# Queries of a pooled-attention and expert-attention kernel loaded as two head halves, with the whole order written anew

## The chip, the cores and the metric

One core of a Trainium2 chip. The metric is the device time of one execution in microseconds, lower is better; the kernel before has a median of 171.48 us over 4 runs (171.14 to 173.48).

## What is computed

Two stages on 8 batches of 576 tokens. Stage one is attention of 8 heads of width 64 in which keys and values are first averaged over 8 neighbours, so that 72 pooled keys remain. Its output, the 8 heads side by side, is the 512-wide input x of stage two: four causal attention "experts" with one head each of width 64, of which a gate picks two for each token.

```
k_p = k.reshape(B, H, Sp, pool, D).mean(axis=3)          # pool = 8, Sp = 72
v_p = v.reshape(B, H, Sp, pool, D).mean(axis=3)
attn = softmax(scale * q @ k_p^T);  x = attn @ v_p       # heads side by side: B x 576 x 512
...
logits = x @ w_gate                                      # 4 experts, the best 2 kept, softmax over them
for e in range(E):
    q, k, v = x @ wq[e], x @ wk[e], x @ wv[e]
    a = softmax(causal(scale * q @ k^T))
    out += (w of e, or 0) * (a @ v @ wo[e])
```

## The kernel before

**An order written out.** The program is a list of some 1,040 tokens, the string SEQ (from L550). A loop at the end of the kernel reads one token after the other and records its instructions; each engine then runs its own instructions in just that order, and semaphores carry what depends on other engines. A token is a step, its batch behind the colon, the PSUM bank behind @, a d for "evict on VectorE (DVE) rather than ScalarE (ACT)", and a c for "cut into four strips of 32 output partitions".

**Steps of stage one, per batch.** Three loads each of k and v, and four of q (load, L114 to L122): all are issued by GpSimd (POOL), which casts float32 to bf16 on the way. PK and PV pool keys and values by a matmul with a small matrix; kc and vc evict; KT and kt transpose the pooled keys. U turns one half of the queries (turn, L253, a DVE transpose by blocks of 32; there are two halves, four heads each). E multiplies turned queries with pooled keys: four pieces a batch, Exy with half x, and four banks each. es, the token e, takes the exponential on ACT (L269). D sums it, d takes the logarithm and x the exponential of its negative (L295, L299), which is the reciprocal. O multiplies with pooled values and o scales into xT on DVE (L310, L317).

**Steps of stage two, per batch.** P makes q and k of the experts, V makes v and the gate's logits, p and v evict them (ACT or DVE). g0 to g9 are the gate: g0 on ACT, g7 (den, L376) and g8 on DVE, the others on POOL (L352 to L383). S makes scores, s the exponential (ACT, L432 or L426), a masks the causal part on POOL (L449, L441), B multiplies with v, bz, bg and b normalise (bg on POOL, L483), T and t transpose, Y multiplies with wo, y evicts and sends out. W0 to W4 load the weights on POOL; c0 to c4 bring them into the order that matmuls need. H are matmuls on zeros, which keep TensorE busy where it has nothing to do.

**What sets the order of the loads.** All loads stand in POOL's own queue, between masks and gate steps. There are three buffers each for q, k and v (NRAW), so a load of batch b waits for the reader of batch b - 3. And there are eight semaphores for POOL's transfers, used in turn: a load waits until the eighth load before it has landed, and what stands behind it in POOL's queue waits with it. The buffer is laid out so that head 4e + r and tokens 18p to 18p + 17 stand in partition 32r + p, place e.

```
def turn(b, i):
    nc.vector.transpose(
        out=qTs[b % 2][:, i].rearrange("p s x u -> p (s x u)").bitcast(U32),
        in_=qraws[b % NRAW][:, i].rearrange("p s d -> p (s d)").bitcast(U32),
    )
```

Before the change, load c of a batch fills partitions 32c to 32c + 31 for both places e, so that each turn needs all four loads of its batch.

Of the kernel before, what the change touches and what calls it, by code (L numbers as in the profile page):

```python
# [20 lines left out]
def kernel(  # L21
# [32 lines left out]
    NRAW = 3  # L54
# [59 lines left out]
    def load(b, nm, c):  # L114
        if nm == "q":
            dst = qraws[b % NRAW][32 * c : 32 * c + 32].rearrange("p e s d -> p e (s d)")
            src = q[b, c::NRG, :, :].rearrange("e (p s) d -> p e (s d)", s=NTK)
        else:
            raw, T = (kraws, k) if nm == "k" else (vraws, v)
            dst = raw[b % NRAW][:, c, :, :, :].rearrange("p h t d -> p h (t d)")  # L120
            src = T[b, :, 2 * KR * c : 2 * KR * (c + 1), :].rearrange("h (p t) d -> p h (t d)", t=2)
        nc.gpsimd.dma_start(out=dst, in_=src)  # L122
# [412 lines left out]
    def z(b, c, queue):  # L535
# [15 lines left out]
        I:0 L_k1:0 L_k2:0 L_k0:0 J:0 K:0 H16:0@7 PK:0@2 kc:0 H4:0@7 KT:0@7 kt:0 L_q2:0 L_q3:0 L_q0:0  # L551
        L_q1:0 U0:0 H7:0@6 E00:0@4 L_q1:1 L_k2:1 L_k0:1 L_k1:1 L_q3:1 L_q0:1 e00:0 E01:0@0 U1:0
        E11:0@4 e01:0 D0:0@0 e11:0 d0:0 x0:0 PK:1@1 kc:1d L_q2:1 E10:0@4 H2:0@3 KT:1@2 e10:0 H4:0@3
        D1:0@4 kt:1 U1:1 E10:1@0 L_v2:0 d1:0 L_v1:0 H2:0@7 E11:1@4 e10:1 U0:1 E01:1@0 e11:1 e01:1
        D2:0@4 d2:0 L_v0:0 PV:0@5 W3:0 vc:0 D1:1@6 E00:1@0 x1:0 M:0 H1:0@7 O11:0@5 O01:0@4 o11:0
        d1:1 L_v0:1 e00:1 L_v1:1 O10:0@7 o10:0 O00:0@6 o00:0 L_v2:1 PV:1@5 vc:1 W0:0 D0:1@2 c0:0d
        H3:0@7 O20:1@5 W1:0 L_k1:2 W2:0 o01:0 x2:0 O11:1@6 d0:1 c1:0 c2:0d O00:1@3 O01:1@0 x0:1
        o00:1 D2:1@2 d2:1 O10:1@1 o01:1 x1:1 x2:1 L_k2:2 c3:0 P_q0:0@4c o20:1 p_q0:0 P_k0:0@2c
        O20:0@3 o20:0 p_k0:0 o10:1 P_q1:0@7c o11:1 L_k0:2 c4:0 L_q1:2 S00:0@2 P_t0:0@5c L_q0:2
        P_k1:0@4c L_q3:2 L_q2:2 p_t0:0d L_q1:3 V1:0@5c p_q1:0d PK:2@7 s00:0 p_k1:0 S12:0@3 S10:0@1  # L560
        kc:2d L_k1:3 V0:0@6 L_k0:3 v1:0d s12:0 v0:0d L_k2:3 KT:2@7 V2:0@0 kt:2d U0:2 L_q3:3 L_v1:2
        s10:0 L_q2:3 L_q0:3 S03:0@3 s03:0 L_k1:4 V3:0@5 v3:0 L_v0:2 S02:0@6 v2:0d L_v2:2 g0:0 g1:0
        E01:2@1 V0:1@5 P_k0:1@0 e01:2 E00:2@1 s02:0 v0:1d L_v1:3 p_k0:1d P_k1:1@5 U1:2 p_k1:1d e00:2
        S11:0@6 PK:3@0 L_v0:3 E10:2@1 s11:0 a00:0 kc:3d P_q1:1@5c L_v2:3 e10:2 D0:2@0 p_q1:1d KT:3@6
        E11:2@1 L_q1:4 a11:0 L_k2:4 P_t0:1@7 d0:2 L_k0:4 V4:1@0 V1:1@5 kt:3d L_q2:4 U0:3 p_t0:1d
        v1:1d e11:2 E00:3@1 x0:2 L_q3:4 v4:1 S01:0@6 V2:1@0 V3:1@5 U1:3 g2:0 v2:1d e00:3 E10:3@1
        s01:0 v3:1d L_q0:4 e10:3 L_q1:5 PV:2@0 D2:2@5 D1:2@6 d1:2 g1:1 d2:2 L_v0:4 P_q0:1@7c x1:2
        E01:3@1 e01:3 L_v1:4 vc:2d L_q0:5 O11:2@0 p_q0:1d o11:2 S12:1@5 L_k2:5 O00:2@7 O10:2@0
        L_k0:6 o00:2 D0:3@1 s12:1 o10:2 g3:0 O01:2@2 o01:2 g4:0 g5:0 g6:0 L_v2:4 d0:3 PV:3@3 E11:3@4
        x2:2 vc:3d L_v2:6 g7:0 S10:1@0 P_q1:2@2c p_q1:2d e11:3 L_k2:6 a01:0 a03:0 g8:0 s10:1 a10:0  # L570
        O20:2@3 S03:1@4 s03:1 D1:3@6 x0:3 o20:2 PK:4@7 kc:4d S01:1@0 s01:1 g2:1 g3:1 g4:1 a12:1
        S00:1@4 V2:2@3 v2:2d P_t0:2@2 V3:2@7 KT:4@3 s00:1 S11:1@0 p_t0:2d d1:3 L_q3:5 P_k0:2@2 s11:1
        U0:4 g0:1 kt:4d E00:4@3 a01:1 v3:2d e00:4 g5:1 g6:1 O01:3@7 D2:3@0 d2:3 P_k1:2@1c L_k0:5
        p_k0:2d x1:3 O00:3@2 g9:0 o01:3 O10:3@7 p_k1:2 g7:1 L_q1:6 E01:4@3 L_q0:6 U1:4 a12:0
        P_q0:2@0c g8:1 O11:3@1 a02:0 o10:3 e01:4 V1:2@7c o00:3 E11:4@3 V0:2@2c o11:3 V1:3@1c p_q0:2d
        L_q2:5 x2:3 L_k1:5 L_q3:7 e11:4 L_q3:6 a11:1 v0:2d v1:3d v1:2d V2:3@0c O20:3@2 g9:1 E10:4@3
        v2:3d e10:4 o20:3 B11:0@1 bz11:0 B01:0@7 bz01:0 bg01:0 B10:0@2 bg11:0 S02:1@3 S03:2@5 s03:2
        P_k0:3@0c s02:1 bz10:0 bg10:0 b10:0 D1:4@5 L_q2:7 V0:3@6c a00:1 L_k1:6 L_v2:5 PV:4@2 PK:5@3
        d1:4 L_v0:5 p_k0:3 v0:3 b11:0 U1:5 S12:2@4 s12:2 x1:4 b01:0 L_v1:5 vc:4d kc:5d S02:2@0
        S10:2@6 s10:2 a02:1 V3:3@2 V4:3@3 v4:3d B00:0@4 s02:2 bz00:0 bg00:0 v3:3d P_k1:3@5 T1:0@3  # L580
        D0:4@6 d0:4 a10:1 g0:3 PK:6@2 D2:4@7 L_v1:7 d2:4 b00:0 S01:2@0 s01:2 t1:0d S11:2@3 T0:0@6
        t0:0 a03:1 B11:1@7 kc:6d s11:2 p_k1:3d B01:1@2 x0:4 a02:2 x2:4 KT:5@5 g1:2 g2:2 P_q0:3@0
        bz11:1 bz01:1 P_t0:3@1 kt:5d E11:5@3 bg11:1 b11:1 p_t0:3 bg01:1 L_q2:6 B00:1@7 p_q0:3d b01:1
        L_v2:7 e11:5 S02:3@0 s02:3 g3:2 g1:3 g2:3 P_q1:3@2 bz00:1 bg00:1 U0:5 b00:1 a10:2 p_q1:3d
        g0:2 a01:2 E01:5@3 g4:2 L_q1:7 KT:6@7 kt:6d O00:4@0 o00:4 g3:3 g4:3 S01:3@1 O01:4@7 e01:5
        o01:4 L_k2:7 L_v0:6 L_k1:7 s01:3 E00:5@3 e00:5 O10:4@0 o10:4 S00:2@1 s00:2 O20:4@7 o20:4
        L_k0:7 O11:4@0 o11:4 E10:5@3 B10:1@7 U1:6 S12:3@1 e10:5 T0:1@0 a11:2 bz10:1 s12:3 E10:6@3
        e10:6 t0:1d PV:5@0 g5:2 S10:3@1 s10:3 bg10:1 g6:2 b10:1 vc:5d V0:4@7 v0:4d g5:3 a12:2
        E11:6@3 g6:3 P_t0:4@0c p_t0:4d e11:6 U0:6 D1:5@2 D0:5@1 d0:5 V1:4@7c V3:4@0c d1:5 S03:3@3
        v1:4d v3:4 S11:3@5 D1:6@1 D2:5@2 V2:4@7c v2:4d P_q0:4@0c s03:3 d1:6 L_q0:7 W4:0 U0:7 d2:5  # L590
        s11:3 p_q0:4d E00:6@1 e00:6 L_v0:7 PK:7@7 g7:2 g8:2 kc:7d O11:5@5 P_k1:4@6c p_k1:4d x0:5
        L_v1:6 x1:5 x2:5 E01:6@0 e01:6 g7:3 P_k0:4@7c o11:5 p_k0:4d O01:5@6 g1:4 g2:4 g8:3 PV:6@4
        vc:6 O20:5@5 D0:6@0 a00:2 o01:5 g9:3 O10:5@1 d0:6 O00:5@7 o10:5 S00:3@2 s00:3 g9:2 Y0:0@4
        a03:2 B01:2@0 o20:5 KT:7@5 o00:5 B00:2@1 bz00:2 y0:0 bz01:2 S03:4@6 S02:4@2 g3:4 g4:4 kt:7d
        a03:3 U1:7 a01:3 bg00:2 P_q1:4@4 g0:4 bg01:2 b01:2 x0:6 B11:2@5 bz11:2 s02:4 b00:2 a02:3
        bg11:2 T1:1@2 b11:2 a02:4 p_q1:4 s03:4 x1:6 B10:2@0 bz10:2 bg10:2 S10:4@3 s10:4 S01:4@6
        t1:1d V1:5@1c b10:2 V2:5@5c V3:5@2c v2:5d v1:5d v3:5d D2:6@3 V0:5@0c O01:6@5 PV:7@4 s01:4
        d2:6 a10:3 V4:5@7c vc:7d a11:3 v0:5 v4:5 E11:7@0 e11:7 o01:6 O11:6@6 o11:6 O00:6@4 o00:6
        Y2:1@7c y2:1 P_q0:5@5c p_q0:5d g5:4 g6:4 E00:7@0 g0:5 g1:5 S12:4@6 a10:4 a00:3 g2:5 g7:4
        P_k0:5@4 p_k0:5d e00:7 s12:4 T1:2@5 t1:2d T0:2@0 t0:2 g8:4 Y2:0@1 S00:4@2 S11:4@6 s00:4  # L600
        P_t0:5@5c y2:0d O10:6@0 P_q1:5@1c p_t0:5 o10:6 E01:7@2 s11:4 Y1:1@0 y1:1d B10:3@7 bz10:3
        p_q1:5 e01:7 a11:4 Y1:0@1 y1:0d a12:3 bg10:3 b10:3 Y0:2@6 y0:2d E10:7@2 B11:3@0 bz11:3
        bg11:3 B01:3@1 e10:7 bz01:3 B00:3@7 bz00:3 b11:3 Y0:1@6 y0:1d x2:6 S00:5@2 s00:5 D0:7@4
        bg01:3 Y2:2@0c bg00:3 b00:3 O01:7@5 V1:6@6c O20:6@7 D1:7@2 g3:5 g4:5 d0:7 O00:7@3 x0:7 y2:2d
        v1:6d d1:7 x1:7 b01:3 O10:7@0 o01:7 o00:7 O11:7@4 P_k1:6@6c D2:7@2 P_k1:5@1c V2:6@3c g5:5
        p_k1:5 o11:7 d2:7 g6:5 g7:5 g8:5 V0:6@4c o20:6 V3:6@5c p_k1:6 a00:4 S11:5@1 o10:7 S10:5@6
        v3:6d v0:6 v2:6d g1:6 s11:5 g9:5 P_t0:6@0 s10:5 a10:5 T0:3@4 t0:3d a11:5 T1:3@3 t1:3 x2:7
        a03:4 P_q0:6@5 S03:5@1 S01:5@6 Y3:2@4c V3:7@3c p_q0:6d O20:7@5 p_t0:6 y3:2 P_q1:6@0c o20:7
        Y4:1@5c P_k0:6@4c a12:4 s03:5 p_q1:6d a00:5 S02:5@0 s01:5 p_k0:6d S12:5@6 a01:5 v3:7 g0:6
        Y3:0@3 V1:7@2 s12:5 g2:6 g9:4 v1:7d B11:4@4 bz11:4 a01:4 s02:5 V4:7@6 y4:1d V0:7@2 v0:7  # L610
        bg11:4 b11:4 B10:4@7 S11:6@0 bz10:4 S01:6@4 bg10:4 B01:4@2 v4:7d g3:6 g4:6 g5:6 P_t0:7@6
        y3:0d bz01:4 bg01:4 s11:6 V2:7@3 v2:7 g1:7 Y3:1@0 b10:4 a03:5 g2:7 g3:7 a12:5 y3:1d B00:4@7
        s01:6 b01:4 P_k0:7@1 g0:7 Y0:3@0 bz00:4 S02:6@2 p_t0:7 S10:6@4 g6:6 T1:4@6 bg00:4 y0:3
        p_k0:7d a02:5 Y2:3@1 P_q0:7@0 b00:4 T0:4@7 s02:6 a11:6 s10:6 Y4:3@2 y2:3d B00:5@4 g7:6 t1:4
        p_q0:7d y4:3d B01:5@5 S00:7@0 S00:6@2 g8:6 bz00:5 B10:5@6 g4:7 bz01:5 bg01:5 b01:5 bg00:5
        b00:5 bz10:5 t0:4 Y1:4@7 bg10:5 b10:5 Y3:3@5 y1:4d a10:6 Y3:4@4 s00:6 y3:4d B11:5@2 P_k1:7@3
# [80 lines left out]
```

## Time and profile before

| | us |
|---|---|
| median of 4 runs | 171.48 |
| the profiled execution | 169.94 |
| its span, first to last instruction | 168.2 |
| busy in it: PE, ACT, DVE, POOL | 153.4, 133.3, 110.4, 108.5 |
| granted TensorE clock, mean over the span | 0.986 |
| POOL's transfers: q | 32 of 144 KB, 6.4 from issue to landing |
| k, v | 24 each of 192 KB, 6.0 and 6.4 |

The page's span runs from the first to the last instruction of the program. PE's share counts overlapping matmuls once and their ends are modelled, so that a full PE is not a PE at its peak; the starts of its matmuls say more. In the slices of the page each digit stands for 4.2 us. In the chain and in the waits, "X <- Y" means that X stood still until Y ended. DMA engines are fed by POOL (loads) and by SP and ACT (stores).

### The profile page before, as it was taken

What the parts mean: (1) busy time and instruction counts of PE and PEld (TensorE: products, weight loads), DVE (VectorE), ACT (ScalarE), POOL (GpSimd) and SP (SyncE); (2) the same over time, 40 slices, a digit from 0 to 9 for tenths busy, and PEclk for the clock granted to TensorE, in tenths of its full rate; (3) what the DMA queues carried; (4) which work ended last, traced back from release to release, by engine and by line L of the source; (5) the groups of instructions that cost most, each with busy time, mean ns of one, the idle gap of its engine ahead of it and who ended that gap; (6) DMA issues with size and microseconds to landing.
All of it is one profiled execution on the core that took longest, in us unless ns stands there. A gap on an engine that the chain in (4) does not pass through costs nothing.

```text
span 168.2 us, 6329 instructions
## 1 busy us (share of the span) xinstructions
PE 153.4 (91%) x2625; PEld 84.4 (50%) x2625; DVE 110.4 (66%) x291; ACT 133.3 (79%) x226; POOL 108.5 (64%) x262
## 2 busy tenths in 40 slices
PE   7775979989999797999999999999999999999970
PEld 2233333454543544756556557645666676546740
DVE  1112707857778668678897797875994677768760
ACT  3028699959999985589999999887779769699870
POOL 7967983598858899999999336513406356556500
PEclk9999699999999999999999999999999999999998
DMA  2999999999999998999999901012610144377785
GB/s 22 175 181 194 180 179 181 202 186 191 182 188 196 182 142 108 142 152 159 102 115 145 156 9 68 4 62 85 234 69 4 62 127 183 99 264 280 241 334 171
DMA packets 49132, 25.05 MB, mean 149 GB/s; under 512 B 42192, under 2 KB 42448, under 8 KB 49104
## 3 DMA queue, kind: packets, MB, share of 16 engines
q0 software_dynamic: 43856, 15.21, 79.8%
q1 hardware_dynamic: 5168, 9.31, 15.6%
q8 instruction: 20, 0.33, 0.7%
q10 hardware_dynamic: 80, 0.13, 0.4%
q14 instruction: 8, 0.07, 0.1%
HBM read 30.42 MB, written 9.44 MB: 237 GB/s over the span
## 4 chain that ended last, share of the span: by engine, by line
PE 58%; DMA 15%; POOL 11%; ACT 8%; issue 3%; DVE 2%; DVEq 0%; POOLq 0%
PE psum L191 52%; DMA qraw<-in_q_dram 9%; DMA kraw<-in_k_dram 6%; ACT eta L269 5%; POOL kraw L122 4%; PE psum L200 3%; PE psum L262 3%; ACT etb L432 2%; POOL etb L449 2%; POOL qraw L122 2%; POOL vraw L122 1%; DVE qT L253 1%; PE psum L179 0%; ACT rza L295 0%; POOL msk L367 0%
## 5 line engine op out<-in xcount | busy, mean ns | idle before, releaser
L432 ACT ACTIVATE etb<-psum 128x1024 bf16<-128x1024 f32 x48 | 48.2, 1028 | 5.1 <-PE psum L191 4.4
L269 ACT ACTIVATE eta<-psum 96x1152 bf16<-96x1152 f32 x32 | 35.8, 1132 | 6.8 <-PE psum L262 6.6
L449 POOL TENSOR_SCALAR_AFFINE_SELECT etb<-etb 128x256 bf16<-128x256 bf16 x64 | 24.9, 406 | 8.3 <-ACT etb L432 7.7
L317 DVE TENSOR_TENSOR xT<-psum,rza 128x512 bf16<-128x512 f32 x32 | 20.6, 682 | 6.4 <-PE psum L191 4.5
L191 PE MATMUL psum<-wvg,xT 128*32 128x260 bf16 (+1 forms) x372 | 20.9, 275 | 2.0 <-DVE xT L317 1.2
L122 POOL DMA_DIRECT2D kraw<-in_k_dram x24 | 18.9, 793 | 4.3 <-PE psum L191 2.0
L182 DVE CAST qk<-psum 128x512 bf16<-128x512 f32 (+1 forms) x26 | 16.7, 646 | 6.6 <-PE psum L191 6.2
L191 PE MATMUL psum<-xT,wkp 128*32 128x512 bf16 (+3 forms) x308 | 20.0, 298 | 0.8 <-issue 0.8
L122 POOL DMA_DIRECT2D qraw<-in_q_dram x32 | 17.5, 550 | 4.8 <-DMA vraw<-in_v_dram 1.3
L122 POOL DMA_DIRECT2D vraw<-in_v_dram x24 | 18.6, 780 | 3.1 <-PE psum L262 1.2
L191 PE MATMUL psum<-wop,oT 128*128 128x512 bf16 (+2 forms) x98 | 20.1, 375 | 0.0
L191 PE MATMUL psum<-xT,wqp 128*32 128x512 bf16 (+3 forms) x320 | 19.8, 301 | 0.0
L191 PEld LDWEIGHTS <-etb 128*128 128x128 bf16 x480 | 17.3, 97 | 4.7 <-issue 2.0
L191 PE MATMUL psum<-vaug,etb 128*128 128x65 bf16 x480 | 19.0, 193 | 0.0
L488 DVE TENSOR_TENSOR osc<-psum,gt 128x256 bf16<-128x256 f32 (+2 forms) x36 | 15.5, 441 | 3.1 <-POOL gt L483 3.1
L191 PEld LDWEIGHTS <-xT 128*32 128x32 bf16 (+1 forms) x372 | 14.0, 96 | 6.9 <-issue 4.4
L191 PE MATMUL psum<-qk 64*128 64x64 bf16 (+4 forms) x192 | 17.3, 278 | 0.1
L262 PE MATMUL psum<-qT,kpT 32*96 32x288 bf16 x256 | 15.0, 309 | 2.4 <-ACT eta L269 1.5
L253 DVE STREAM_TRANSPOSE qT<-qraw 128x576 uint32<-128x576 uint32 x16 | 12.1, 764 | 7.8 <-DMA qraw<-in_q_dram 7.8
L483 POOL TENSOR_TENSOR gt<-rzb,G 128x4 f32<-128x4 f32 (+2 forms) x36 | 6.9, 201 | 14.2 <-DVE rzb L481 13.8
L182 DVE COPY ofin<-psum 128x512 f32<-128x512 f32 (+1 forms) x20 | 13.4, 674 | 3.4 <-PE psum L191 2.6
L179 PE MATMUL psum<-warm 128*128 128x512 bf16 x39 | 13.6, 498 | 1.2 <-DVE onesd L150 1.2
(78 smaller groups left out, 234.6 us busy)
## 6 DMA issues: line engine op xcount, KB each, us to landing
out_dram<-ofin SPq DMA_DIRECT2D x32, 256.0 KB, 2.2
kraw<-in_k_dram POOLq DMA_DIRECT2D x24, 192.0 KB, 6.0
qraw<-in_q_dram POOLq DMA_DIRECT2D x32, 144.0 KB, 6.4
vraw<-in_v_dram POOLq DMA_DIRECT2D x24, 192.0 KB, 6.4
out_dram<-ofin SPq DMA_DIRECT2D x7, 128.0 KB, 2.3
oT<-in_moe_wq_dram POOLq DMA_DIRECT2D x1, 256.0 KB, 7.6
oT<-in_moe_wk_dram POOLq DMA_DIRECT2D x1, 256.0 KB, 8.2
oT<-in_moe_wv_dram POOLq DMA_DIRECT2D x1, 256.0 KB, 8.6
```

The costliest lines, as they stand in the source:

```text
L122: nc.gpsimd.dma_start(out=dst, in_=src)
L179: nc.tensor.matmul(out=psum[:, bank, :], lhsT=warm[:, 0:128], rhs=warm[:], start=True, stop=True)
L182: (nc.vector.tensor_copy if dve else nc.scalar.copy)(out=out, in_=in_)
L191: nc.tensor.matmul(out=out, lhsT=lhsT, rhs=rhs, start=start, stop=stop)
L253: nc.vector.transpose(out=qTs[b % 2][:, i].rearrange("p s x u -> p (s x u)").bitcast(U32), in_=qraws[b % NRAW][:, i].rearrange("p s d -> p ...
L262: nc.tensor.matmul(out=psum[0:KR, bank + r, 0 : HALF].rearrange("j (s x) -> j s x", s=NTK), lhsT=kpTs[b % 2][rows, u, i, :], rhs=qTs[b % 2 ...
L269: nc.scalar.activation(out=etas[b % 2][:, NRG * i : NRG * i + NRG, HALF * z : HALF * z + HALF].rearrange("j r (x s) -> j r x s", s=NTK), i ...
L317: nc.vector.tensor_tensor(out=xT[:, 2 * g + t, mcols(b)], in0=psum[:, bank, :], in1=rz[:, g, 0:MAIN], op=MULT)
L432: nc.scalar.activation(out=et[:, ep, :, eo : eo + n], in_=psum[:, bank : bank + 2, 0:n], func=EXP, scale=MOE_EXP_SCALE,)
L449: nc.gpsimd.affine_select(out=blk, in_=blk, pattern=[[0, 2], [1, 128]], compare_op=ISGE, fill=0.0, base=0, channel_multiplier=-1,)
L483: nc.gpsimd.tensor_mul(out=gt[:, :, :, 0], in0=rz[:, :, :, 0], in1=at[b // 2, "G"][:, p0:p1, 2 * ep : 2 * ep + 2].rearrange("p c e -> p e c"),
L488: nc.vector.tensor_tensor(out=oscs[ep][:, own, :].rearrange("p c (e d) -> p e c d", e=2), in0=o[:, :, :, 0:HD], in1=gt.to_broadcast([128, ...
```

## The change

A load of q is now one half of the heads over all 128 partitions: c is the place e, and one transfer brings heads 4c to 4c + 3. There are two per batch, of 288 KB. Data, layout and all arithmetic are as before.

```diff
         if nm == "q":
-            dst = qraws[b % NRAW][32 * c : 32 * c + 32].rearrange("p e s d -> p e (s d)")
-            src = q[b, c::NRG, :, :].rearrange("e (p s) d -> p e (s d)", s=NTK)
+            dst = qraws[b % NRAW][:, c].rearrange("p s d -> p (s d)")
+            src = q[b, NRG * c : NRG * c + NRG, :, :].rearrange("r (p s) d -> (r p) (s d)", s=NTK)
```

The string SEQ is another one from its first line to its last: other places for loads, matmuls, evictions and gate steps, other banks, and another choice of ACT or DVE for evictions. Its lines that the prediction speaks of (start, first projections, gate of batch 0, k and v of batch 5):

```diff
-        I:0 L_k1:0 L_k2:0 L_k0:0 J:0 K:0 H16:0@7 PK:0@2 kc:0 H4:0@7 KT:0@7 kt:0 L_q2:0 L_q3:0 L_q0:0
-        L_q1:0 U0:0 H7:0@6 E00:0@4 L_q1:1 L_k2:1 L_k0:1 L_k1:1 L_q3:1 L_q0:1 e00:0 E01:0@0 U1:0
...
-        o00:1 D2:1@2 d2:1 O10:1@1 o01:1 x1:1 x2:1 L_k2:2 c3:0 P_q0:0@4c o20:1 p_q0:0 P_k0:0@2c
...
-        L_k0:6 o00:2 D0:3@1 s12:1 o10:2 g3:0 O01:2@2 o01:2 g4:0 g5:0 g6:0 L_v2:4 d0:3 PV:3@3 E11:3@4
-        x2:2 vc:3d L_v2:6 g7:0 S10:1@0 P_q1:2@2c p_q1:2d e11:3 L_k2:6 a01:0 a03:0 g8:0 s10:1 a10:0
...
-        L_q2:5 x2:3 L_k1:5 L_q3:7 e11:4 L_q3:6 a11:1 v0:2d v1:3d v1:2d V2:3@0c O20:3@2 g9:1 E10:4@3
+        I:0 L_k1:0 M:0 J:0 K:0 L_k2:0 L_k0:0 H16:0@7 PK:0@6 kc:0 H4:0@7 KT:0@6 L_q1:0 U1:0 L_k2:1
+        kt:0d H3:0@7 E11:0@0 L_q0:0 U0:0 L_k0:1 E10:0@4 e11:0 e10:0 E01:0@0 e01:0 D1:0@4 L_k1:1
+        PK:1@5 L_q0:1 U0:1 kc:1 E00:0@0 d1:0 H2:0@7 KT:1@5 e00:0 kt:1d H3:0@7 E01:1@4 L_q1:1 U1:1
...
+        W1:0 o01:0 O20:0@5 O11:0@6 L_q0:2 o11:0 H2:0@3 PK:2@4 W0:0 d0:1 x2:0 L_q1:2 O00:0@7 o00:0
+        kc:2 H3:0@3 KT:2@4 W3:0 c2:0d x0:1 W2:0 P_k0:0@7 kt:2d c3:0 L_v1:1 d2:1 P_k1:0@0 L_v0:1 U0:2
...
+        O11:3@4 a00:0 v3:2 e00:4 L_q1:6 P_q1:2@7c p_q1:2 o11:3 L_q1:5 g5:0 g6:0 g7:0 g8:0 D1:4@5
...
+        L_v0:7 s00:2 P_k1:3@3 x1:5 T0:0@0 KT:6@6 U0:6 g4:2 p_k1:3d a10:1 kt:6d t0:0d L_v0:5 B10:1@7
+        bz10:1 V0:4@4 v0:4 L_v2:7 B11:1@6 bz11:1 E10:6@0 e10:6 bg10:1 b10:1 V2:3@5c bg11:1 PV:5@4
+        a02:1 v2:3 b11:1 V4:3@7c PK:7@6 E01:6@0 v4:3 g0:3 vc:5d O20:5@4 x2:5 o20:5 e01:6 V2:4@7c
```

Warm-up matmuls on zeros are 36 in all, where they were 39.

## The prediction

> **What bounds the kernel now.** I read the slices of the page first, then the chain of waits in order of time, then the list of waits of the whole span, then the timeline around the two longest idle pieces of TensorE.
>
> ```profile
> PE   7775979989999797999999999999999999999970
> ACT  3028699959999985589999999887779769699870
> POOL 7967983598858899999999336513406356556500
> PEclk9999699999999999999999999999999999999998
> DMA  2999999999999998999999901012610144377785
> ```
>
> That is the page's table of 40 slices of 4.2 us. DMA is full from slice 2 to 16 and after: loads are served without a break up to about 62 us. PE has gaps up to slice 16 and hardly any later. ACT is full from 38 to 58 us (slices 10 to 13) and from 76 to 102.
>
> ```profile
> 11.30 6.55 DMA qraw<-in_q_dram
> ...
> 45.06 8.01 DMA qraw<-in_q_dram
> ...
> 55.95 0.20 POOL d L372
> ...
> 67.79 4.74 DMA kraw<-in_k_dram
> ...
> 117.71 8.85 PE psum L191 x218
> ```
>
> The chain, in order of time: up to 72.5 us it runs through loads and POOL, later through PE alone. The page puts 58% on PE, 15% on DMA, 11% on POOL. So the last 96 us are TensorE's own work, and a change can gain only by letting that work start earlier or by closing gaps before about 100 us.
>
> ```profile
> DVE den L376 <- POOL d L372: 3.8, 2, 2.0
> PE psum L191 <- DVE xT L317: 1.4, 2, 1.2
> PE psum L191 <- DVE xT L310: 0.9, 1, 0.9
> PE psum L262 <- ACT eta L269: 1.5, 3, 1.0
> ```
>
> Waits (sum, count, longest). The first three lines are one story. POOL's queue holds the gate steps behind loads that wait for one of the eight transfer lanes, so d is late; DVE stands at den for 2.0 and 1.75 us; behind den stand the xT products, and PE waits for those:
>
> ```profile
> 56.18 0.17 DVE L376 SCALAR_TENSOR_TENSOR den<-d 128x4 f32<-128x4 f32 x1 [2.04 <-POOL d L372]
> 57.40 0.61 PE L191 MATMUL psum<-wvg,xT 128*128 128x260 bf16 x4 [0.89 <-DVE xT L310]
> ```
>
> **A ledger of TensorE.** In 100 to 160 us, where PE never waits, the distance from one step's first matmul to the next one's (timeline) is 0.87 us for P, 0.45 for V, 0.43 for Y, 0.31 for S, 0.40 for E, 0.22 for O and D. Over all steps of the order that is 131.9 us: P 31.8, V 16.2, Y 15.6, S 15.5, B 15.1, E 12.9, the rest 24.8. The real span up to the last matmul is 163.2, so 31 us are lost: 20.8 before the first projection (P_q0:0 starts at 28.99 with 8.2 of the ledger done), 10.5 after. With "mark n" for the place where n us of the ledger are done, mark 15 is passed at 36.9 us and mark 75 at 105.2: 68.3 us for 60 us of work.
>
> **The change part by part.**
>
> Query loads. 32 transfers of 32 partitions become 16 of 128, with the same rows of 2304 B in SBUF. POOL's issue is 533 ns for 64 rows (median) and 769 for the 768 rows of a v load; 128 rows lie between, nearer the first: 0.56. 32 x 0.55 - 16 x 0.56 = 8.6 us less on POOL (112.8 to 104 of summed instructions). On the transfer side quarters land 0.72 us apart, so a half takes 1.45; 128 rows at the 81 rows per us of the trace would be 1.58. I take 1.45: no bandwidth is gained. The Trainium skill ("DMA: Bandwidth & Descriptors", "Anatomy of one DMA") gives a transfer a fixed 2 us, which with sixteen fewer would promise up to 32 us. The row decides: landings 0.72 us apart at 6.4 us each say that the fixed part is overlapped. By the rule -32, by the row 0; I count 0.
>
> Start. A turn U now needs one half and not four quarters. k of batch 0 lands at 8.8 us as now; one q half is next, at about 10.3 (where two quarters have landed now: 10.29); kp and kpT are ready at 11.2, U1 at 11.2 and E11 runs at 11.6 instead of 12.77. The first exponential starts near 12.0, not 13.29. Then I follow the rows: ACT has eight E exponentials (1.13 each, 1.05 when back to back), kp, three logs, two x, vp; the loads of k1, q1, v0 end at 21 us as now (21.16), the same bytes. v0 to vp to O to xT (0.68 each on DVE) gives the first projection at 28.0 with 7.5 of the ledger done. The weights wk land about 25.9, wq at 28.9 (now 27.46 and 25.94), wv at 32 (30.05), v of batch 1 at 35.3 (now 24.5): that last is pushed behind k2, q2 and all weights, and its reader PV:1 now stands at ledger 14.5, reached about 35.4. So it just fits. Mark 15 comes at 35.9 instead of 36.9: -1.0.
>
> Warm-up matmuls: 36 instead of 39, all in idle places: 0. The row PEclk shows one slice at 6: the granted clock is 0.5 for 3.4 us from 16.7, where PE waits for data anyway. The Trainium skill ("TensorE: Matmul & The Clock Gate", Part 1) says that a window of about 3.4 us without work halves the clock and as long a busy one restores it; that speaks against fewer warm-ups. By the rule one more halved window over dense work would cost 1.7; by the row such a window falls into the start, cost 0. I take 0 and keep 1.7 for the range.
>
> The gates. They stood at ledger 28 to 30 (batch 0) and were executed 6 us late. Now g5:0 to g8:0 stand at 36.3, right behind L_q1:5, whose lane by the same count of bytes is free near 55 to 57 us, while PE gets there near 58. If that holds, both waits at den go: the 0.89 and 1.2 us of PE (-2.1). What is late next is G, whose first reader, the scaling of B10:0, stands 2.3 us of ledger after it.
>
> Other gaps. L_k1:5 ends 4.7 us before its PK:5, with 0.46 us of PE lost; now k of batch 5 is issued 11.5 us of ledger ahead: -0.5. In 83 to 90 us ACT alternates one E and one S exponential while E00, E01, E10 of batch 5 and 6 share banks 3 to 6: in the ledger PE is 2.5 us behind there. In the new order the steps between ledger 40 and 110 stand farther from the reader of their bank than that reader lasts (0.1 us is missing in all); I take 1.5 of the 2.5: -1.5.
>
> What it costs. (a) ACT: by the order and the rows ACT takes over 5 kp, 6 V and 6 Y evictions and gives away 9 oT, 2 kpT and 2 weight copies: +1.4 us, DVE -4.8. More important is where: between marks 15 and 75 ACT now has 74.4 us of summed instructions, before 72.1. Busy time is 0.88 of such sums (133.3 of 151.9), so 65.5 against 63.4: +2.1, and ACT is nearly full there. Between 0 (hidden) and 2.1 I take 2.1. (b) L_v0:5 stands 2.2 us of ledger before PV:5, behind two other loads; v loads took at least 4.9 us from issue to landing (the tile's own view). Short by up to 2.7; from 0 (PE late anyway) to 2.7, I take 1.5. V and P queue behind it in PE. (c) The tail (Y, last stores) has the same shape: 0.
>
> Sum: -1.0 - 2.1 - 0.5 - 1.5 + 2.1 + 1.5 = -1.5. The profiled execution took 169.94 us, 168.2 of them span; it is 1.5 below the median of the four runs shown (171.48). The same 1.5 off the span gives a span of 166.7, and off the median 170.0.
>
> **The rivals.**
>
> Slower: ACT stays as idle as it was. Before, the stretch from mark 15 to 75 took 68.3 us with 63.4 of ACT in it, 4.9 idle. With the same 4.9 the new one takes 70.4, and mark 75 comes at 106.3, 1.1 late though the start gained 1.0; PV:5 adds 1.5. +2.6: 174.1. For it: ACT at 9.8 of 10 in 40 to 60 us, and the new order puts 14.6 us of summed ACT work beside marks 15 to 25, where it was 11.8. Against: ACT's long waits (6.6 us for E) are mostly in the start. It decides for slower once ACT idles over 3.4 us there.
>
> Faster by more: ACT's extra work is hidden and v of batch 5 is in time: -5.1, 166.4. For it: POOL has 8.6 us less to issue. Against: DMA is full until 62 us.
>
> Nothing: the loads in total are the bound up to 62 us, same bytes; all gains before are waited away: 171.3. That the change doesn't do what it says can be left out: the order shows 128x1152 transfers, eight unwaited.
>
> **How the numbers follow.** Forecast 0.45 (170.0, own range 168.5 to 171.4), slower rival 0.30, faster rival 0.20, nothing 0.05. One per cent, about what a measurement of this kernel can tell from none, is 1.7 us: bounds 169.8 and 173.2. Faster: 0.20 + 0.20 of the forecast = 0.40. Same: 0.25 + 0.05 = 0.30. Slower 0.30. The range goes to the rivals' centres, 166.4 to 174.1, leaving out about 0.1 at each end, with the clock's 1.7 inside it.
>
> **What would show it.** First E matmul near 11.6 us, first projection near 28; the line "DVE den <- POOL d" gone or under 1 us; no PE wait on kraw near PK:5; a PE wait on vraw of 1 to 2 us around 80 us; POOL near 100 us busy; ACT busy 134 to 135. Wrong if ACT's idle between marks 15 and 75 exceeds 3.4 us, if a second slice of PEclk is low, or if PV:1 waits past 36 us.

## The result and the profile after

| | before | after |
|---|---|---|
| median, us | 171.23 (63 runs, 169.76 to 173.82) | 169.83 (44 runs, 165.08 to 172.48) |
| ratio of the comparison | | 0.9719, 95% interval 0.9692 to 0.9746 |
| the profiled execution; its span | 169.94; 168.2 | 170.28; 168.6 |
| busy PE, ACT, DVE, POOL | 153.4, 133.3, 110.4, 108.5 | 154.2, 134.3, 106.9, 100.7 |
| mean granted clock in the profile | 0.986 | 0.958 |

The comparison leaves disturbed runs out, and of the changed kernel's 44 it keeps only those near its fastest, so that its ratio (faster by 2.8%) and the medians (0.8%) do not say the same. The reason lies in the kernel: its 44 executions form two groups. 11 have a mean granted clock of 0.98 or more and took 165.1 to 167.9 us; 33 have 0.938 to 0.976 and took 168.0 to 172.5. The profiled execution is of the second group, and shows where the time goes there. The slices of its page (compare PEclk with the row of before):

```profile
PE   7576959999989999999989999999999999999980
...
ACT  3027694789989999999989999888889586799880
POOL 7956664605979998699177755309636717463610
PEclk9997595799999999999999999999999999999999
DMA  2999999993999999999949950400013175468885
```

Before had one slice of low clock, from 16.7 to 20.1 us. Here there are two stretches. The second lies in slices 6 and 7, counted from 0, and there the first projections are due. The table by stretches (columns after the bounds: length, busy times, then the granted clock in the sixth place) has it exactly: 24.75 to 31.57 us ran at half clock.

```profile
24.75:31.57 6.82, 6.82 (x56) 1.93 (x56) 2.87 (x5) 3.90 (x9) 3.44 (x6) 0.50 1.57 191
```

TensorE's timeline there (start, length, tile, count):

```profile
30.34 1.41 PE L179 MATMUL psum<-warm 128*128 128x512 bf16 x3
31.59 0.34 PE L200 MATMUL psum<-ident,kp 96*128 96x96 bf16 x4
31.76 1.89 PE L191 MATMUL psum<-xT,wkp 128*128 128x512 bf16 x8
```

The three matmuls on zeros between PK:2 and KT:2 take 1.4 us of TensorE's queue, and P_k0:0 starts at 31.76 us, where the prediction had 28.0 and before 28.99. The list of waits answers to the one of before:

```profile
POOL etb L449 <- ACT etb L432: 17.5, 7, 7.3
...
PE psum L191 <- DMA kraw<-in_k_dram: 2.5, 1, 2.5
...
PE psum L262 <- ACT eta L269: 1.3, 2, 0.8
```

DVE's 3.8 us at den and PE's waits for xT are gone from it. POOL's waits at masks have grown (before: 7.7 us in four, the longest 5.6): a10:0 stands in POOL's queue ahead of seven loads and waits 7.3 us for ACT's exponential (run e7 below).

In marks of the prediction's ledger, before and after (counted anew in each profile; the prediction's own count for before was 36.9 and 105.2): mark 15 at 37.41 and 40.66, mark 75 at 105.51 and 106.78, the last matmul at 163.15 and 163.71. So the changed kernel lost 3.25 us up to mark 15 and won 2.0 between 15 and 75 and 0.7 behind it.

### The profile page after: what moved, and what is told of

Its sections match the earlier page's. It is cut to its first block, busy times and chain, and to the rows that moved or that the text cites. A ratio compares the mean times of both kernels' runs of the same rounds, so it can differ in the third digit from the quotient of the medians.

```text
span 168.6 us, 6081 instructions
## 1 busy us (share of the span) xinstructions
PE 154.2 (91%) x2502; PEld 83.9 (50%) x2502; DVE 106.9 (63%) x284; ACT 134.3 (80%) x233; POOL 100.7 (60%) x246
## 4 chain that ended last, share of the span: by engine, by line
PE 80%; ACT 7%; DMA 5%; POOL 2%; DVE 1%; issue 1%; POOLq 0%; DVEq 0%
PE psum L191 67%; PE psum L262 6%; ACT eta L269 5%; DMA qraw<-in_q_dram 5%; PE psum L200 4%; PE psum L179 3%; POOL kraw L122 2%; ACT etb L432 1%; ACT rza L299 1%; ACT qk L182 0%; DVE qT L253 0%; POOL qraw L122 0%; DVE vaug L182 0%; DVE ofin L182 0%; POOL diff L154 0%
## 5 line engine op out<-in xcount | busy, mean ns | idle before, releaser
L432 ACT ACTIVATE etb<-psum 128x1024 bf16<-128x1024 f32 x48 | 47.5, 1032 | 4.0 <-PE psum L191 3.6
L449 POOL TENSOR_SCALAR_AFFINE_SELECT etb<-etb 128x256 bf16<-128x256 bf16 x64 | 25.0, 406 | 17.7 <-ACT etb L432 17.5
L317 DVE TENSOR_TENSOR xT<-psum,rza 128x512 bf16<-128x512 f32 x32 | 21.2, 683 | 11.9 <-PE psum L191 11.8
L191 PE MATMUL psum<-wvg,xT 128*32 128x260 bf16 (+1 forms) x348 | 22.4, 275 | 0.0
L191 PE MATMUL psum<-wop,oT 128*32 128x512 bf16 (+2 forms) x122 | 20.7, 377 | 0.0
L191 PEld LDWEIGHTS <-etb 128*128 128x128 bf16 x480 | 18.1, 97 | 4.7 <-issue 1.7
L191 PE MATMUL psum<-vaug,etb 128*128 128x65 bf16 x480 | 20.1, 193 | 0.0
L262 PE MATMUL psum<-qT,kpT 32*96 32x288 bf16 x256 | 15.6, 321 | 4.8 <-DVE qT L253 1.7
L191 PE MATMUL psum<-qk 64*128 64x64 bf16 (+4 forms) x192 | 16.6, 277 | 0.1
L182 ACT COPY ofin<-psum 128x512 f32<-128x512 f32 (+1 forms) x23 | 12.8, 582 | 3.7 <-PE psum L191 3.3
L191 PE MATMUL psum<-eta,vp 96*32 96x512 bf16 (+1 forms) x256 | 15.4, 306 | 0.0
```

What stands on the lines that cost most here:

```text
L182: (nc.vector.tensor_copy if dve else nc.scalar.copy)(out=out, in_=in_)
L191: nc.tensor.matmul(out=out, lhsT=lhsT, rhs=rhs, start=start, stop=stop)
L262: nc.tensor.matmul(out=psum[0:KR, bank + r, 0 : HALF].rearrange("j (s x) -> j s x", s=NTK), lhsT=kpTs[b % 2][rows, u, i, :], rhs=qTs[b % 2 ...
L317: nc.vector.tensor_tensor(out=xT[:, 2 * g + t, mcols(b)], in0=psum[:, bank, :], in1=rz[:, g, 0:MAIN], op=MULT)
L432: nc.scalar.activation(out=et[:, ep, :, eo : eo + n], in_=psum[:, bank : bank + 2, 0:n], func=EXP, scale=MOE_EXP_SCALE,)
L449: nc.gpsimd.affine_select(out=blk, in_=blk, pattern=[[0, 2], [1, 128]], compare_op=ISGE, fill=0.0, base=0, channel_multiplier=-1,)
```

## The experiments

Medians of each run with those of before from the same set:

| run | what | us | before | clock |
|---|---|---|---|---|
| e1_again, e12_again | the changed kernel | 169.73, 169.99 | 171.50, 171.12 | 0.946 to 0.990 |
| e2 | old order, halves | 168.16 | 171.50 | 0.985 to 0.995 |
| e9 | e2 and 16 small extra loads | 173.28 | 171.12 | 0.973 to 0.985 |
| e4 | new order, quarters | 173.85 | 171.50 | 0.927 to 0.986 |
| e6, e5 | den late: old order, e2 | 170.86, 169.93 | 171.04 | 0.975 to 1.000, 0.968 to 0.995 |
| e7 | changed, two masks moved | 169.57 | 171.04 | 0.939 to 0.983 |
| e3 | changed, 14 more warm-ups | 171.79 | 171.50 | 0.956 to 0.997 |
| e8 | changed, 20 of 36 warm-ups | 168.16 | 171.04 | 0.921 to 0.945 |
| e11 | changed, 28 of 36 | 169.58 | 171.12 | 0.944 to 0.977 |
| e10, e15 | changed, no warm-up | 167.68, 166.78 | 171.12, 170.94 | (see below) |
| e13 | e2, no warm-up | 169.24 | 170.94 | |
| e14 | before, no warm-up | 170.57 | 170.94 | |

**What do the loads alone do? (e2)** The old order, in which each batch's first and third quarter are dropped and the second and fourth become the half that its first and second turn need:

```diff
-L_q2:0 L_q3:0 L_q0:0 L_q1:0 U0:0 H7:0@6 E00:0@4 L_q1:1 L_k2:1 L_k0:1 L_k1:1 L_q3:1 L_q0:1
+L_q0:0 L_q1:0 U0:0 H7:0@6 E00:0@4 L_k2:1 L_k0:1 L_k1:1 L_q1:1
```

> The old order with the new loads only: each batch's second and fourth quarter load become the two halves, the first and third are taken out. Theory that the new order makes the gain: no change against the kernel before, within 0.7 us, since the bytes are the same and land no earlier; at most 1 us less where POOL's freed 8.6 us brings the gate steps forward and DVE's waits at den (3.8 us) shrink. Rival, that the larger transfers make the gain: 3 to 5 us less, as with the whole change.

168.16 us, ratio 0.9824 (0.9773 to 0.9875): 3.3 us for the loads alone, where I expected 1 at most, and 1.6 us less than the whole change has in the same set (169.73). Lines of its page: the waits, and the DMA issues (KB each, us to landing).

```profile
DVE den L376 <- POOL d L372: 1.2, 2, 0.8
...
PE psum L191 <- DVE xT L317: 0.3, 1, 0.3
```

```profile
qraw<-in_q_dram POOLq DMA_DIRECT2D x16, 288.0 KB, 8.0
```

The two gate waits fell from 3.8 to 1.2 us with the gates left in their place: POOL, 100.6 us busy in place of 108.5, reaches d in time. Each transfer takes longer than a quarter did (8.0 us against 6.4), and the gain is there all the same. Mark 15 comes 1.2 us earlier, mark 40 3.35 (63.64 against 66.99), the last matmul 2.4.

**Is it the size of a load or the number of them? (e9)** As e2, with a small load that nobody reads where the dropped quarters stood:

```diff
+    extras = bufs(16, [32, 2, D], BF16, "extra")
...
-        if nm == "q":
+        if nm == "q" and c > 1:
+            dst = extras[2 * b + c - 2][:]
+            src = q[b, c::NRG, 0:32, :].rearrange("e p d -> p e d")
+        elif nm == "q":
...
-L_q0:0 L_q1:0 U0:0
+L_q2:0 L_q0:0 L_q3:0 L_q1:0 U0:0
```

> The order before with the new loads (halves in the place of each batch's second and fourth quarter, as in the run with halves in the old order, 168.2), and in the place of the first and third quarter a load of 64 rows of 256 bytes into a tile that nobody reads (16 in all, 16 KB each from memory): the same number of transfers on POOL's queue, and of turns of the eight semaphores, as before, with nearly the bytes of the halves alone. It parts two causes that the halves have together. Theory (what pays is that 16 issues and 16 turns of the eight semaphores are gone): the gain is lost again, POOL busy near 108 us, den's wait back over 2.5 us, 170.5 to 171.5. Rival (what pays is that a turn now waits for one large load, placed early, and that fewer separate transfers share the engines): the gain stays, 168 to 169.

The gain is gone and 2 us more: 173.28, ratio 1.0173 (1.0112 to 1.0234). The waits and the extra loads:

```profile
DVE den L380 <- POOL d L376: 4.5, 2, 3.1
...
PE psum L195 <- DVE xT L314: 2.0, 1, 2.0
```

```profile
extra<-in_q_dram POOLq DMA_DIRECT2D x16, 8.0 KB, 5.9
```

A load of 8 KB takes 0.53 to 0.60 us of POOL's queue, nearly as much as a large one (0.56 to 0.64), and holds its place among the eight in flight for 5.9 us: 15 of the 16 land 0.15 to 0.21 us after the load issued just ahead of them. Against e2, each relative to its own before, 16 transfers cost 5.5 us, 0.34 each. (That e9 ends above before and not at it I can't explain in full: its two waits at den are 4.5 us where before had 3.8.) So the number of loads in POOL's queue pays, not the bytes. How much of it is POOL's time for issuing and how much the turn among the eight, no run separates.

**Does the new order need the large loads? (e4)** The changed kernel, each half as two transfers of 64 partitions:

```diff
-            dst = qraws[b % NRAW][:, c].rearrange("p s d -> p (s d)")
...
-        nc.gpsimd.dma_start(out=dst, in_=src)
+            for i in range(2):
+                dst = qraws[b % NRAW][64 * i : 64 * i + 64, c].rearrange("p s d -> p (s d)")
...
+                nc.gpsimd.dma_start(out=dst, in_=src)
```

> The new order with each half loaded as two transfers of 64 partitions: 32 query loads again, two lanes of the eight taken where one was. Theory that the new order counts on eight transfers in flight of this size: POOL has 8 us more to issue and its loads wait longer for a lane, gate steps come later, 1 to 3 us slower than the changed kernel. Rival, that lanes and issue time are hidden: as the changed kernel, within 0.7 us.

173.85, ratio 1.0122 (1.0035 to 1.0209), 4 us above the changed kernel. The new order alone is a loss; it lives on sixteen turns fewer.

**What is the place of the gates worth? (e6, e5)** g7 and g8 of batches 0 and 1 moved down to just before g9, in the kernel before (e6) and in e2 (e5):

```diff
-... g7:0 ... g8:0 ... O00:3@2 g9:0
+... O00:3@2 g7:0 g8:0 g9:0
```

> The kernel before with nothing changed but g7 and g8 of batches 0 and 1, which are moved down to just before g9. It prices the prediction's step on the gates (-2.1 us). Theory: PE's two waits for xT (1.4 and 0.9 us) go, and about 2 us with them: ratio 0.985 to 0.992. Rival (what stands behind is late too, since the loads that made POOL late are still there; the gain in the old order came from the loads alone): under 0.7 us, ratio 0.996 to 1.0.

0.9984 (0.9951 to 1.0016): nothing. The wait at den is gone from its list and mark 40 comes 2.6 us earlier than in before, but at 45 it is 0.6 late. TensorE's timeline between says where it went:

```profile
65.59 0.27 PE L191 MATMUL psum<-vaug,etb 128*128 128x65 bf16 x3
67.72 2.38 PE L191 MATMUL psum<-vaug,etb 128*128 128x65 bf16 x45 [1.86 <-POOL etb L449]
```

B now waits 1.86 us for a mask of the late POOL, and from 68.44 the granted clock is halved for 3.4 us in that execution. The cause (POOL late behind its loads) stayed and the wait moved; of the 3.2 us lost between these marks it is 1.86, and 3.4 us at half clock are enough for the rest.

> The order before with only the new loads (two halves a batch, each in the place of the second and fourth quarter), and g7 and g8 (the logs' sums and the gate's product) of batches 0 and 1 moved down to just before g9. Together with the next run it makes a table of two by two: quarters or halves, den early or late. Theory (larger loads pay through POOL's time, and den late pays only what POOL's lateness still costs): with halves den's wait is 1.2 us already, so this move brings 0.5 to 1.5 us more than the halves alone had (168.2): about 167, ratio 0.970 to 0.982. Rival (the two are independent and add up): the full 2.1 us, 166 or less.

169.93, ratio 0.9769 (0.9712 to 0.9826): it parted into executions of 166.6 to 169.2 at a clock of 0.99 and of 170.6 to 171.7 at 0.968 to 0.979. Both expectations missed its median; it shows no gain over e2 and settles no more.

**Does the hole in the transfers cost anything? (e7)** In the changed kernel, POOL's timeline:

```profile
32.08 0.57 POOL L122 DMA_DIRECT2D qraw<-in_q_dram  x1
39.99 0.41 POOL L449 TENSOR_SCALAR_AFFINE_SELECT etb<-etb 128x256 bf16<-128x256 bf16 x1 [7.34 <-ACT etb L432]
40.36 1.56 POOL L122 DMA_DIRECT2D vraw<-in_v_dram  x2
```

No load is issued for 8 us. The edit moves a10:0 behind L_k2:4 and a02:0 behind L_q1:4:

```diff
-E11:2@0 s10:0 a10:0 e11:2 D0:2@7
+E11:2@0 s10:0 e11:2 D0:2@7
...
-L_k2:4 kc:3 s01:0 S12:0@1 U1:3 a02:0
+L_k2:4 a10:0 kc:3 s01:0 S12:0@1 U1:3
```

> The changed kernel with two masks moved in POOL's queue: the first mask of batch 0 behind the loads it holds back (down to behind the second k load of batch 4), the next mask behind q's load of batch 4. In the profile of the changed kernel POOL stands 7 us at that mask and the transfers run dry for one or two slices. Theory (PE's own work and the clock set the time there, loads have slack): no change, within 1 us of the changed kernel's median in this set. Rival (the hole in the transfers is paid later by PE, when loads of batches 2 to 4 come late): 1.5 to 3 us less.

169.57, that is 1.5 us below before of its set, where e1 is 1.8 and e12 1.1 below theirs: no change. In e7's profile no load is held up there any more, so the hole was slack.

**Is it the clock, and can warm-ups mend it? (e1, e3)**

> The changed kernel unchanged, for a second profile and the clock of each execution. Clock theory: an execution with a mean granted clock of 0.98 or more has at most one halved stretch of 3.4 us before 21 us and a span near 164 us; one near 0.95 has a second halved stretch between 21 and 32 us and a span near 168.5 us, so times fall into two groups some 4 us apart. Rival (the order alone sets the time, the clock is a by-product): spans do not follow the clock, the spread is as that of the kernel before, 1 us or so. Where the stretch is undisturbed, ledger mark 15 comes at 36 us and mark 75 near 102 us, as the sum of the prediction without its costs has it.

169.73; the same two groups: 166.88 us at a clock of 0.990, 168.8 to 170.8 at 0.946 to 0.966.

> The changed kernel with 11 more matmuls on zeros in the idle places from 11 to 28 us (47 instead of 36). Clock theory: the halved stretch at 21 to 32 us becomes rare, more executions have a mean clock of 0.98, and the median falls by 2 to 4 us against the changed kernel; the fastest executions stay as they are, near 165.5 us. Rival, that the slower executions have another cause: median as the changed kernel, or up to 1 us more for the added matmuls.

The edit adds matmuls on zeros in seven places, 14 of them (50 in all; the expectation counts 11 and 47), such as

```diff
-D1:0@4 L_k1:1 PK:1@5 L_q0:1
+D1:0@4 H2:0@7 L_k1:1 PK:1@5 H2:0@7 L_q0:1
```

171.79, 2 us above the changed kernel, where I expected 2 to 4 below. Its profile has three halved stretches (from 10.9, 17.7 and 24.6 us, the last of 6.8 us), and at half clock each zero matmul cost 0.43 us of TensorE's queue. So I turned it round.

**Fewer warm-ups (e8, e11, e10, e12)**

> The changed kernel with its first 20 warm-up matmuls kept and the later 16 left out. Clock theory (the start's mean load on TensorE decides whether its clock is halved, and the halved clock over the first projections is what makes most executions of the changed kernel 3 to 4 us slower than its best): the good executions get rarer or vanish, the granted clock's mean lies under 0.96 and the median 0.5 to 3 us above the changed kernel's. Rival (the warm-ups themselves are in the way at half clock, 0.43 us each, and the clock falls whatever they do): 0.5 to 2 us less.

> The changed kernel with the last 8 of its 36 warm-ups left out, those that stand right before the pooling of batch 2's keys and the first projections (they took 3 us of TensorE's queue there at half clock). Clock theory: the halving of 21 to 31 us is decided by what lies before, so the clock stays in two groups as in the changed kernel; but the executions at half clock lose less: median 1 to 2 us under the changed kernel in this set. Rival (the waits for keys of batch 2 set the first projections, the warm-ups only fill them): no change, within 0.7 us.

> The changed kernel without any of the 36 warm-up matmuls. With the later 16 left out the start ran at half clock for 17 us, but at the full clock from 27.4 us on, and the first projection came at 29.2 in place of 31.8. Theory (what counts is only that the clock is full when projections begin, and at half clock the start's own work fills its windows and brings the clock back by itself): within 1 us of the run with 20 warm-ups (168.2), so faster than or equal to the changed kernel. Rival (the first 20 carry the start: without them its E pieces run at half clock from the first, ACT's exponentials begin 1 to 2 us later and the whole chain with them): 1 to 2.5 us above that run.

> The changed kernel once more, as a measure for the two runs beside it on the same chip. As before: two groups of times, at a mean granted clock over 0.98 near 166 us and at 0.94 to 0.97 near 170 us, the median between 168.5 and 170.5.

```diff
-H16:0@7 PK:0@6 kc:0 H4:0@7 KT:0@6 ... H3:0@7 E11:0@0 ... H2:0@3 PK:2@4 ... H3:0@3 KT:2@4
+PK:0@6 kc:0 KT:0@6 ... E11:0@0 ... PK:2@4 ... KT:2@4
```

(e10; e8 keeps H16 and H4, e11 keeps all but the last eight matmuls on zeros.) e8: 168.16, ratio 0.9849 (0.9808 to 0.9891), and its granted clock is half from 10.3 to 27.4 us, yet its first projection starts at 29.19 against 31.76. A lower mean clock, and a better time: my clock theory in this form (the mean decides) fell. e11 changed the median by 0.4 us and kept the two groups (165.2 and 165.6 at a clock of 0.977, 169.3 to 171.1 at 0.944 to 0.949): its clock theory missed, its rival held. Its four executions at the low clock were not profiled, so why leaving out those eight did not help them stays open. e10, with none, beat the changed kernel of the same set by 2.3 us.

**Does that hold in the old order? (e13, e14, e15)** The same edit in e2, in the kernel before, and e10 again:

> The order before with the new loads and without any of its 39 warm-ups. The run of the changed kernel without any showed matmuls of 512 columns 427 ns apart up to 31.9 us (half clock, which its records do not show, since they begin there), and still an earlier first projection than with warm-ups. Theory (warm-ups cost queue time and bring nothing before the first projections, in any order): at or below the halves with warm-ups (168.2): 166.5 to 168.2. Rival (in the old order the warm-ups do their work, the first projections stand at 27 to 31 us and would now run at half clock): 1 to 3 us above, 169 to 171.

> The kernel before without any of its 39 warm-ups. Theory (they bring nothing in any order): the same as before within 1 us, 170 to 171.5. Rival (they do their work in the old order): 172 to 174.

> The changed kernel without any warm-up once more, to rank it against the halves in the old order without any, in the same set. It was 167.7 (164.8 to 169.6) beside 170.0 for the changed kernel. Theory: 167 to 168.3 again, one group, ratio to before 0.975 to 0.985.

e14: 0.9976 (0.9945 to 1.0008), no change; e13: 169.24, 1.1 us above e2, but from six executions each, in two sets, whose ranges overlap (167.8 to 170.5 and 167.5 to 170.1). In e14's profile the first projections do lack the clock that the warm-ups of before bring: 1.3 us at mark 15, gone again by mark 40 (67.04 and 66.99). Timelines of before and of e14, the same matmuls:

```profile
28.99 1.04 PE L191 MATMUL psum<-xT,wqp 128*32 128x512 bf16 x16
29.86 1.04 PE L191 MATMUL psum<-xT,wkp 128*32 128x512 bf16 x16
```

```profile
29.90 1.93 PE L191 MATMUL psum<-xT,wqp 128*32 128x512 bf16 x16
31.61 1.79 PE L191 MATMUL psum<-xT,wkp 128*32 128x512 bf16 x16
```

From start to start 0.87 us and 1.71: half clock, though e14's records show none (last section).

e15: 166.78, ratio 0.9775 (0.9714 to 0.9836). Its slices and the first projection:

```profile
PE   0037788999999999999999999999999999999980
...
ACT  3017898899999999998998999698887784899780
```

```profile
28.21 1.90 PE L191 MATMUL psum<-xT,wkp 128*128 128x512 bf16 x8 [0.29 <-DVE wkp L182]
30.04 0.47 PE L262 MATMUL psum<-qT,kpT 32*96 32x288 bf16 x8
```

28.21 us where the prediction had 28.0, and 3.5 before the changed kernel's. Mark 15 comes at 36.99, mark 75 at 102.20, the last matmul at 159.13. e10's profile, of an execution of 169.58 us, is in step with it up to PK:2 (26.07 and 26.22 us), but at half clock until 31.95:

```profile
28.99 3.14 PE L191 MATMUL psum<-xT,wkp 128*128 128x512 bf16 x7 [0.62 <-DVE kpT L182]
```

Its mark 15 comes at 39.0. So two things cost time here. The half clock over the first projections takes 2.0 us up to mark 15, without any warm-up (e10 against e15). And matmuls on zeros take 0.43 us each where they run at half clock: with two of them before KT:1 and six between KT:1 and PK:2, PK:2 starts at 28.8 to 29.2 us in the profiles of the changed kernel, e1, e12 and e7, and at 26.07 in e10, which is at half clock too. Of that, 1.6 us are left at mark 15 (39.0 against 40.66 in the changed kernel) and 0.7 at the last matmul (163.04 against 163.71).

The 12 executions of e10 and e15 have a median of 167.3 us, the 12 of e1 and e12 169.9. By that the changed kernel without its warm-ups is the best version found: 2.6 us below the changed kernel, about 3.7 below before, 0.9 below e2. It is no faster than the changed kernel's 11 executions at the high clock (median 166.5, though these are picked by their clock): what it has is fewer slow ones (2 of 12 above 169 us, where e1 and e12 have 9 of 12).

## Why the prediction was wrong

**The step that failed is the pair of costs, (a) and (b).** The sum set 3.6 us of them against the gains, and they were measured at nothing; without them it is -5.1, close to the 4.8 of the comparison. The gains came out near their total by luck, since their parts were wrong: the loads, put at 0, gave 3.3 us, and the gates, k of batch 5 and the stretch of 83 to 90 us, put at 4.1 together, added 1.7.

It said -1.5 us; the comparison says -2.8%, some 4.8 of 171.2. The side was right, and of its cases the rival that was faster by more (166.4) is where its executions at the high clock lie. None of those was profiled; the nearest profile is e11's, with eight matmuls on zeros fewer: marks 15, 75 and end at 37.10, 102.10 and 159.03, that is -0.3, -3.1 and -0.7 against before.

- **"Query loads ... I count 0".** The first step that was mis-sized. It weighed bandwidth and a transfer's latency, rightly found no gain there, and priced 8.6 us of POOL's time at nothing. e2 measured -3.3 us, and e9 took it away by number alone. The Trainium skill's fixed 2 us a transfer ("DMA: Bandwidth & Descriptors", "Anatomy of one DMA") would have promised 32; the runs show 0.2 (e2 against before) to 0.34 us a transfer (e9 against e2), paid in POOL's queue and in turns of the eight in flight.
- **"The gates" (-2.1).** The waits did go, as said, but the place of g7 and g8 did not do it: e6 alone gives nothing. The wait came from POOL's lateness, and fewer loads alone mend it (e2: 1.2 us left of 3.8). It was the loads' gain, entered under another name.
- **Costs (a) and (b), +2.1 and +1.5: both measured at nothing.** ACT was busy 63.5 us between marks 15 and 75 (62.4 before) and idle 2.6 where it had been idle 5.7: the extra work went into idle time, and the slower rival fell with it, below its own limit of 3.4. v of batch 5 landed at 85.98, 0.9 us before PV:5 at 86.88. Had both stood at 0, the sum would have been -5.1, the faster rival's.
- **"L_k1:5 ... -0.5" and the stretch of 83 to 90 us, -1.5.** PE does not wait at PK:5 (66.42; its loads landed by 62.9). From mark 55 to 65 TensorE took 11.4 us in place of 12.1: 0.7 of the 1.5. What the new order adds to the loads in all is 1.7 us (last matmul at 159.03 in e11, 160.76 in e2), against 4.1 that gates, k of batch 5 and this stretch were given.
- **The start, -1.0.** E11 ran at 11.80 (11.6 predicted). But mark 15 came at 40.66, not 35.9, since the next point went wrong. Where the clock is full from 6.8 to 68 us, in e4's profile (the same order and warm-ups, each half in two transfers), the first projection starts at 27.63 (28.0 predicted) and mark 15 at 36.8; without warm-ups, in e15, at 36.99. That is 0.6 and 0.4 us before the 37.41 of the kernel before: the path was right, its worth about half.
- **"Warm-up matmuls ... 0", with 1.7 kept for the range.** A second low slice of PEclk was named as what would make the forecast wrong, and it is there. The reading behind the 0 was off too: in the halved stretch of before PE did not wait for data but ran six matmuls on zeros (2.9 of 3.4 us), and e14, without them, reaches D1:0 1.3 us earlier. So the rule's price of 1.7 for one more halved window over dense work was nearer than my 0 (e10 against e15: 2.0). Its remedy is not borne out: fourteen warm-ups more made the kernel 2 us slower (e3), none at all 2.6 us faster at the median. The profiles show warm-ups at half clock in the queue before the first projections; that they are the whole of the 2.6 is not shown, since e11, without the last eight, gained 0.4. The median of all runs (169.83) lies near the 170.0 by luck: this loss offsets the costs that did not come.
- **The tail, 0.** 0.7 us better behind mark 75. No run took that apart.

Left open: what decides between the two groups of the changed kernel, and when the full clock comes back in e10 and e15. The first record of full clock stands at 6.09 us in e11's profile, and at 4.27, 4.60, 5.38 and 5.64 in those of the changed kernel, e7, e1 and e12, which were all at half clock from 24.8 to 29.2 us. That a window of the clock runs freely of the kernel's start, as the skill says ("TensorE: Matmul & The Clock Gate", Part 1), would fit; no run here tests it. Loading v of batch 5 earlier was not run either.

## What to carry over

A transfer costs a turn in the queue that issues it, and what stands behind it pays: count issues and turns, not only bytes, and when a wait is read off a list, ask what made its source late before crediting the place of the waiter. Test warm-ups by taking them out: at half clock each took 0.43 us of TensorE's queue here, and a set of them that changes nothing in one order (e14) can cost 2.6 us in the next. When executions of one kernel part into two groups, look at which group the profile is from before reading it, and compare like with like: the changed kernel is 4.8 us below before in its best executions and 1.4 at the median of all.

## What the runs showed of the hardware

**The clock's records begin late.** In the profile of before the 16 first matmuls on zeros stand together:

```profile
1.24 6.17 PE L179 MATMUL psum<-warm 128*128 128x512 bf16 x16 [1.24 <-DVE onesd L150]
```

Start to start they are 426 ns apart at the median, 216 being the full clock's, and the first record of the clock (full) is at 6.44. In e10 the first record is at 31.95, and P's matmuls of 512 columns are 427 ns apart until then. So TensorE starts at half clock, the row PEclk shows 9 where nothing was recorded, and the mean granted clock of a kernel without warm-ups (0.992 to 1.000) says nothing of its start. That TensorE starts so is in the skill too ("TensorE: Matmul & The Clock Gate", Part 1: the default state is throttled, 426.7 ns for 512 columns).

**A full clock is lost during work, not only in idleness.** In the changed kernel it was taken away at 24.75 us. In the 3.41 us before that TensorE was busy for 1.83, and never idle for longer than 0.6 at a stretch. In e8 it came back at 27.4 without a matmul on zeros, after 3.41 us in which TensorE was busy throughout: at half clock the same work fills twice the time (427 ns a matmul of 512 columns, where it is 216).
